# Inverses of two of six row tiles on GpSimd, VectorE's kept in PSUM, in a three-part kernel on one core

## The chip, the core and the metric

The kernel runs on one core of one Trainium2 chip. The metric is the device time of one launch in microseconds (us). A time of a profile is that of one execution, counted from the start of its span.

## The reference

Three parts follow one another; the output of one is the input of the next.

```python
# 1. delta rule: 4 batches x 8 heads, S=768 tokens, D=48
for t in range(S):
    y[:, :, t] = einsum('bhd,bhde->bhe', q[:, :, t], state)
    v_old = einsum('bhde,bhd->bhe', state, k_n[:, :, t])
    state = state + beta_t * outer(k_n[:, :, t], v_t - v_old)
# 2. experts: 3072 tokens of 384, 8 experts of 1024, the best one for each token
e_idx = argmax(x @ w_gate + modality_bias[modality_id])
out[mask_e] = gate_w[mask_e] * (relu(x[mask_e] @ w1[e]) @ w2[e])
# 3. dense layer, 384 -> 2048 -> 384, weights given as float64
h = x @ w_in
out = (h * sigmoid(h)) @ w_out
```

## The kernel before

**Attention.** The 768 tokens are six row tiles t = 0..5 of 128 rows; the 32 heads are two halves p of 16. For each tile TensorE finds the products of keys with keys and of queries with keys (`gram`; VectorE masks the latter into `KB`, `keep_reads`, line 347, eight instructions for each tile, called masks below). The delta rule inside a tile needs, for each head, the inverse of unit lower triangular blocks. All 32x32 blocks of a tile stand side by side: `to_lanes` (one 32x32 transpose, line 361) puts them into `L`, `scales` gives the scaled diagonal of the inverse `A`, and `step(t, j)`, j = 0..30, works the inverse out row by row, each step with multiplications into `tmp` and additions into `A`, in two halves so that neighbouring instructions do not depend on each other. `spread` (line 438) transposes `A` back. Then TensorE joins the 32x32 blocks into 64x64 ones (`join`, line 453), and weights, state and outputs of the tile follow (`lower`, `weigh`, `update`, `state`, `read`), with ScalarE keeping each result. Before, VectorE does all six tiles' steps, with `A` in SBUF; GpSimd only clears `A`.

**Router.** After tiles 1, 2, 4 and 5 a `wave` on VectorE takes the logits of the finished tiles, ranks the tokens of each expert and makes the lists of token indices (the work around line 839 to 1126). It uses constants (`lane`, `k128`, `slot`, ...), counted by GpSimd and cast by VectorE.

**Experts.** The first half of the tokens (tiles 0 to 2) is served in five slots of 256 tokens, in 8 chunks of 128 hidden columns each: `first` is nine matrix products in fp32r pieces (line 1252, high and low parts of tokens and weights), relu is ScalarE's, `second` is plain fp32 products (line 1346, four in the trace) into the two PSUM banks `po`. These slots overlap tiles 4 and 5. GpSimd issues the gathers of their tokens (line 1220, `xg`). The second half is served in four slots of 512 tokens, by three fp32r passes (line 1259), each operand split into a high part by ScalarE and a low part by VectorE (line 1216).

**Dense layer.** Six groups of 512 tokens. The float64 weights come in 28 parts, each of which takes VectorE five instructions (lines 1518 to 1527), called fills below.

**The order.** The class `Order` plans all jobs of the attention, the router and slots 0 to 4 (those of 512 tokens come behind): each job has a key, an engine, a cost, jobs that it waits for and a number from PLAN["rank"]; the order in which each engine's instructions are written follows from them. An engine runs its own in the order written. In gaps of TensorE the planner puts `pulse`s, products of ones whose result is never used (line 709).

Of the kernel before, what the change touches and what calls it, by code (L numbers as in the profile page):

```python
# [1862 lines left out]
```

## Time and the profile before

| | us |
|---|---|
| time, median of 3 runs | 936.82 (935.92 to 937.26) |
| time of the profiled execution | 936.33 |
| its span | 934.6 |
| TensorE busy, in the span | 886.9 |
| VectorE busy | 586.4 |
| ScalarE busy | 424.4 |
| GpSimd busy | 84.4 |

The profiled execution's own time stands 1.7 us over its span and 0.5 us under the median. Its mean granted TensorE clock is 0.974 of full. Busy time is the sum over instructions of what an engine worked on; TensorE's contains the pulses. In rows, PE is TensorE, PEld its weight load, DVE VectorE, ACT ScalarE, POOL GpSimd, SP SyncE.

### The profile page before, as it was taken

Reading aid. Unit: us, or ns where it says so; the run is one execution under the profiler, and the core shown is the slowest. Engines: PE = TensorE matmul, PEld = TensorE weight load, DVE = VectorE, ACT = ScalarE, POOL = GpSimd, SP = SyncE. Lnnn points to the kernel's source line nnn. Section 1 sums busy time; section 2 is a strip of 40 time slices with the busy share of each in tenths; the row PEclk is TensorE's granted clock in tenths of the full one; section 3 lists DMA queues with packets and bytes.
Section 4 is the critical chain, followed back from the end, with each engine's and each line's share of the span. In section 5 each row is a group of like instructions: output and inputs, shape, how many; then the busy total and the mean of one; then the engine's idle time right before and its main releaser. Section 6 shows DMA issues by size and latency. Waiting matters only on the chain. (4 is left out here: it accounts for less than half of the span.)

```text
span 934.6 us, 23107 instructions
## 1 busy us (share of the span) xinstructions
PE 886.9 (95%) x9293; PEld 740.8 (79%) x9293; DVE 586.4 (63%) x1671; ACT 424.4 (45%) x832; POOL 84.4 (9%) x85
## 2 busy tenths in 40 slices
PE   7879998987999799999998999999999999999998
PEld 4548888876888577889887888888888888888897
DVE  4999997999934694699963676542443443343332
ACT  4228576854786434456653544332332233233232
POOL 5000000011011134123311000000000000000000
PEclk8899989998999899999998999999999999999999
DMA  8934645646154505565742531030030100100100
GB/s 193 186 103 104 162 101 145 140 114 196 35 138 131 180 9 160 183 224 179 241 152 65 106 78 43 11 58 1 16 53 1 20 15 1 23 11 1 30 6 35
DMA packets 135351, 85.28 MB, mean 91 GB/s; under 512 B 102361, under 2 KB 121447, under 8 KB 135232
## 3 DMA queue, kind: packets, MB, share of 16 engines
q1 hardware_dynamic: 131904, 73.84, 32.0%
q0 software_dynamic: 3328, 9.83, 3.3%
q8 instruction: 76, 1.25, 0.6%
q14 instruction: 43, 0.35, 0.1%
HBM read 70.53 MB, written 14.55 MB: 91 GB/s over the span
## 5 line engine op out<-in xcount | busy, mean ns | idle before, releaser
L1655 PE MATMUL fpo<-fgh,o 128*128 128x512 f32 x480 | 163.0, 396 | 0.0
L1646 DVE TENSOR_TENSOR fq<-fy,fgh 128x512 fp32r<-128x512 f32 x96 | 66.1, 688 | 110.7 <-ACT fgh L1644 105.2
L1642 DVE TENSOR_TENSOR fy<-fph,fy 128x512 f32<-128x512 f32 x96 | 66.2, 690 | 110.2 <-ACT fy L1640 109.9
L1644 ACT CAST fgh<-fy 128x512 fp32r<-128x512 f32 x96 | 59.6, 621 | 130.7 <-PE fpo L1655 99.2
L1640 ACT ACTIVATE fy<-fph 128x512 f32<-128x512 f32 x96 | 57.4, 598 | 124.0 <-PE fph L1637 122.2
L1637 PE MATMUL fph<-fxh,il 128*128 128x512 f32 x288 | 113.4, 394 | 0.0
L1637 PE MATMUL fph<-fxh,ih 128*128 128x512 f32 x288 | 113.3, 393 | 0.0
L1655 PEld LDWEIGHTS fpo<-fgh,o 128*128 128x128 f32 x480 | 90.3, 188 | 21.2
L1655 PE MATMUL fpo<-fq,o 128*128 128x512 f32 x240 | 95.1, 396 | 0.0
L1259 PE MATMUL poe<-w2s,pairs 128*128 128x384 f32 x384 | 78.5, 347 | 4.1 <-ACTq L1490 3.2
L1259 PEld LDWEIGHTS poe<-w2s,pairs 128*128 128x128 f32 x384 | 69.6, 192 | 8.9 <-ACTq L1490 3.5
L416 DVE TENSOR_TENSOR tmp<-A,L 128x126 f32<-128x126 f32 (+20 forms) x336 | 70.5, 251 | 0.9
L422 DVE TENSOR_TENSOR A<-A,tmp 128x126 f32<-128x126 f32 (+20 forms) x336 | 70.3, 250 | 0.0
L1252 PE MATMUL bank<-xh,wRH 128*128 128x256 f32 x240 | 61.0, 331 | 5.7 <-DVE wRH L1308 5.1
L1637 PEld LDWEIGHTS fph<-fxh,ih 128*128 128x128 f32 x288 | 54.2, 188 | 11.9
L1637 PEld LDWEIGHTS fph<-fxh,il 128*128 128x128 f32 x288 | 54.2, 188 | 11.9
L1346 PE MATMUL po<-raw,hs 128*128 128x384 f32 x160 | 62.5, 516 | 0.0
L1637 PE MATMUL fph<-fq,ih 128*128 128x512 f32 x144 | 57.0, 396 | 0.0
L1637 PE MATMUL fph<-fxl,ih 128*128 128x512 f32 x144 | 56.4, 391 | 0.0
L1655 PEld LDWEIGHTS fpo<-fq,o 128*128 128x128 f32 x240 | 45.2, 188 | 10.8
L1252 PEld LDWEIGHTS bank<-xh,wRH 128*128 128x128 f32 x240 | 41.6, 199 | 10.7 <-DVE wRH L1308 5.5
L709 PE MATMUL po<-ones 128*128 128x512 bf16 x103 | 33.3, 428 | 11.7 <-DVE KB L347 5.3
(436 smaller groups left out, 1660.8 us busy)
## 6 DMA issues: line engine op xcount, KB each, us to landing
raw<-in_moe_w_dram SPq DMA_DIRECT2D x72, 384.0 KB
ri<-in_moe_w_in_dram SPq DMA_DIRECT2D x12, 512.0 KB
ro<-in_moe_w_out_dram SPq DMA_DIRECT2D x16, 384.0 KB
vs<-in_vd_dram SPq DMA_DIRECT2D x12, 384.0 KB
KI<-in_kd_dram SPq DMA_DIRECT2D x24, 192.0 KB
Z<-vs SPq DMA_DIRECT2D x24, 192.0 KB
xs<-Y SPq DMA_DIRECT2D x48, 96.0 KB
fy<-ys SPq DMA_DIRECT2D x72, 64.0 KB
```

Source lines behind the costliest of these rows:

```text
L416: nc.vector.tensor_tensor(tv, r[:, :, j : j + 1].to_broadcast([128, c, n]), L[:, j : j + 1, j + 1 :].to_broadcast([128, c, n]), op=ALU.mult,)
L422: nc.vector.tensor_tensor(r[:, :, j + 1 :], r[:, :, j + 1 :], tv, op=ALU.add)
L709: return nc.tensor.matmul(room, dense, dense[:, None, :].to_broadcast([128, 4, 128]), start=True, stop=True).ins
L1252: self.nc.tensor.matmul(ph, a[:, k, :], b[:, k, :], start=(i == 0), stop=(i == 8))
L1259: self.mark = self.nc.tensor.matmul(o, a[:, cs], b, start=(c == 0 and i == 0), stop=(c == self.F - 1 and i == 2)).ins
L1346: nc.tensor.matmul(self.po[b][:, 0:384], v["h"][c % 2][:, 128 * b : 128 * b + 128], self.raw(1, c), start=(c == 0), stop=(c == F - 1),)
L1637: nc.tensor.matmul(ph, a[:, k, fs], b[:, k, :], start=(n == 0), stop=(n == 8))
L1640: nc.scalar.activation(sg, ph, AF.Sigmoid)
L1642: nc.vector.tensor_tensor(gv, ph, sg, op=ALU.mult)
L1644: self.marks = [nc.scalar.copy(gh, gv).ins]
L1646: self.marks.append(nc.vector.tensor_tensor(gl, gv, gh, op=ALU.subtract).ins)
L1655: nc.tensor.matmul(po[k], a[:, rows], b, start=(f == 0 and i == 0), stop=(f == 15 and i == 2))
```

## The change

Tiles 1 and 4 (`lanes="vpvvpv"`) have all their steps, from scaling `L` on, done by GpSimd, with `A` in SBUF and one update of each step (a multiplication into `tmp`, an addition). Tiles 0, 2, 3 and 5 stay on VectorE, but their `A` lies in PSUM, in the experts' two banks `po`: even rows in one, odd rows in the other. TensorE clears them with two products of zeros (`nil`), the diagonal takes two instructions, and `spread` two transposes of half the size. The first product into `po` (slot 0, chunk 0) waits for the spreads of tiles 4 and 5. An update now adds a multiple of one row to the rows below it; before, it was columns.

The counting and casting of the router's constants are jobs of the order, GpSimd's next count waiting for VectorE's cast. Slots 3 and 4 do their second product in three fp32r passes (`passes=(3, 4)`): VectorE makes the low parts of hidden values (`relu_low`) and of weights (`lo(s, c, 1)`), ScalarE the high ones. A pulse has 256 columns in place of 512, and lies in another bank; in the order there are 56 of them, 103 before. All rank numbers, some costs and so the whole order are new.

```diff
-    one=3, pair=(),
+    lanes="vpvvpv", passes=(3, 4),
...
-        kq=198.9, qb=242.4, vs=64.9, kd=1074.8, gr=178.8, gq=-206.4, Gc=265.8, Kc=-543.5, dg=116.5, zero=481.9,
+        kq=-837.5, qb=792.4, vs=95.3, kd=359.6, gr=277.9, gq=1463.3, Gc=-140.5, Kc=-143.2, dg=145.6, zero=168.1,
...
     def clear_inverses(self, t):
-        A = self.st[t]["A"] = self.pools["ln"].tile([128, 32, 32], F32, tag="A", name=f"A{t}", bufs=2)
-        self.nc.gpsimd.memset(A, 0.0)
+        if PLAN["lanes"][t] == "p":
+            A = self.st[t]["A"] = self.pools["ln"].tile([128, 32, 32], F32, tag="A", name=f"A{t}")
+            self.nc.gpsimd.memset(A, 0.0)
+            return
+        self.st[t]["A"] = self.rows
+        for x in self.rows:
+            self.nc.tensor.matmul(
+                x, self.nil, self.dense[:, None, :].to_broadcast([128, 4, 128]), start=True, stop=True
+            )
...
     def step(self, t, j):
...
+        L, A = self.st[t]["L"], self.st[t]["A"]
+        pool = PLAN["lanes"][t] == "p"
+        eng = self.nc.gpsimd if pool else self.nc.vector
...
-        if j < PLAN["one"]:
-            for i in range(j + 1):
-                for L, A in LA:
-                    nc.vector.scalar_tensor_tensor(
-                        A[:, i, j + 1 :], L[:, j, j + 1 :], A[:, i, j : j + 1], A[:, i, j + 1 :], op0=ALU.mult, op1=ALU.add
-                    )
-            return
...
+        c = j + 1
+        if pool:
+            parts = [(A[:, c:, 0:c], A[:, j : j + 1, 0:c], L[:, j, c:, None])]
         else:
-            rows = [(LA[0][0], LA[0][1][:, w : j + 1 : 2]) for w in range(2)]
+            row = A[j % 2][:, j // 2 : j // 2 + 1, 0:c]
+            parts = []
+            for w in (c % 2, j % 2):
+                k = (c + 1 - w) // 2
+                if k < 16:
+                    parts.append((A[w][:, k:, 0:c], row, L[:, j, 2 * k + w :: 2, None]))
...
+            eng.tensor_tensor(tv, row.to_broadcast([128, n, c]), l.to_broadcast([128, n, c]), op=ALU.mult)
             tmps.append(tv)
-        for (_, r), tv in zip(rows, tmps):
-            nc.vector.tensor_tensor(r[:, :, j + 1 :], r[:, :, j + 1 :], tv, op=ALU.add)
+        for (x, _, _), tv in zip(parts, tmps):
+            eng.tensor_tensor(x, x, tv, op=ALU.add)
...
+                add(("st", t, j), "POOL" if PLAN["lanes"][t] == "p" else "DVE", self.step_cost(t, j),
+                    lambda t=t, j=j: self.step(t, j), [("st", t, j - 1)] if j else [("b2", t)])
+            add(("sp", t), "DVE", 2.15, lambda t=t: self.spread(t), [("st", t, 30)])
...
+        for j, (count, cast) in enumerate(router.consts):
+            once(("ci", j), "POOL", 0.25, 0, count, [("cc", j - 1)])
+            once(("cc", j), "DVE", 0.25, 0, cast, [("ci", j)])
...
-            return nc.tensor.matmul(room, dense, dense[:, None, :].to_broadcast([128, 4, 128]), start=True, stop=True).ins
+            return nc.tensor.matmul(room, dense, dense[:, None, :].to_broadcast([128, 2, 128]), start=True, stop=True).ins
...
+        def relu_low(s, c):
+            hh, hl = v["hh"][c % 2], v["hh"][2 + c % 2]
+            nc.vector.scalar_tensor_tensor(hl, v["ph", s, c], 0.0, hh, op0=ALU.max, op1=ALU.subtract)
...
         def second(s, c):
+            if s in PLAN["passes"]:
+                h = v["hh"][c % 2], v["hh"][2 + c % 2]
+                self.second(c, [x[:, 0:384] for x in self.po], *h, self.bufs["h2"][c % 2], self.bufs["l2"][c % 2])
+                return
...
-                    + ([("ev", s - 1, 0, b) for b in range(2)] if s and c == 0 else []) + ([("wv", 2, "idx")] if (s, c) == (0, 0) else []))
+                    + ([("ev", s - 1, 0, b) for b in range(2)] if s and c == 0 else []) + ([("wv", 2, "idx"), ("sp", T - 1), ("sp", T - 2)] if (s, c) == (0, 0) else []))
```

Three places show how the order moves. A row is: source line, operation, output and input names, size, number. First, VectorE at the start of the program (L is the blocks of tile 0, lines 742 to 754 and 770 cast constants, KB are masks). Before:

```order
L742 CAST lane<-lanei 128x128
L742 CAST k_136<-k128i 128x24
L353 COPY G<-G 32x512
L742 CAST k_140<-k256i 128x12
L742 CAST slot<-sloti 128x52
...
L353 COPY G<-G 32x512
L361 STREAM_TRANSPOSE L_309<-G 128x1024
L347 TENSOR_TENSOR KB_106<-bank_128,amask 64x512 x2
L347 TENSOR_TENSOR KB_106<-bank_124,amask 64x512 x2
L347 TENSOR_TENSOR KB_106<-bank_125,amask 64x512 x2
L347 TENSOR_TENSOR KB_106<-bank_126,amask 64x512 x2
L373 RECIPROCAL rn_399<-n_0_354 128x32
```

And with the change:

```order
L770 CAST lane<-lanei 128x128
L770 CAST k_136<-k128i 128x24
L770 CAST k_137<-k256i 128x12
L355 COPY G<-G 32x512
L770 CAST slot<-sloti 128x52
L355 COPY G<-G 32x512
L375 STREAM_TRANSPOSE L_300<-G 128x1024
L770 CAST down<-downi 128x8
L770 CAST V<-tii 128x24
L770 CAST V<-pii 128x24
L387 RECIPROCAL rn_355<-n_0_327 128x32
```

The second copy of diagonals stands ahead of three casts that it stood behind, and the eight masks that stood between L and the first step are gone from there; they and sixteen more now stand behind the spread of tile 0.

Second, GpSimd where it ends tile 4 (A_1374 is its inverse, L_2871 its blocks) and goes on to the first slot's gathers, with the change:

```order
L437 TENSOR_TENSOR tmp_29_0_4070<-A_1374,L_2871 128x60
L440 TENSOR_TENSOR A_1374<-A_1374,tmp_29_0_4070 128x2x30
L437 TENSOR_TENSOR tmp_30_0_4073<-A_1374,L_2871 128x31
L440 TENSOR_TENSOR A_1374<-A_1374,tmp_30_0_4073 128x31
L1246 DMA xg<-xs,gidx_3811 128x384 x6
```

Before, there were only clearings ahead of the same gathers:

```order
L357 MEMSET A_2419 128x1024
L357 MEMSET A_3272 128x1024
L1220 DMA xg<-xs,gidx_3863 128x384 x5
```

So the gathers stand behind the whole of tile 4's 66 instructions.

Third, VectorE in slots 3 and 4 with the change (line 1376 is `relu_low`, 1336 the low part of a weight, 1562 to 1571 are fills); in the order before, no fill stands ahead of the slots of 512 tokens:

```order
L1336 TENSOR_TENSOR pairs<-raw_4265,pairs 128x384
L1376 SCALAR_TENSOR_TENSOR hhl<-bank_127,hhl 128x256
L1336 TENSOR_TENSOR wRH<-raw_4146,wRH 128x384
L1571 TENSOR_TENSOR il<-ri_0f,ih 128x512
L1336 TENSOR_TENSOR pairs<-raw_4265,pairs 128x384
L1562 TENSOR_SCALAR ri_2e<-ri_2_6945 128x512
L1571 TENSOR_TENSOR il<-ri_1f,ih 128x512
L1376 SCALAR_TENSOR_TENSOR hhl<-bank_128,hhl 128x256
```

Each chunk of these slots has three VectorE instructions of its own (before one), and ten of the 28 parts' fills stand between them.

On TensorE, 11 of the gram jobs stand ahead of the first join (before 20), and ahead of the join of tile 5 the experts' chunks are two firsts and no second (before seven firsts and seven seconds).

## Rows read from the trace of the kernel before

**Rows 1.** Six stretches: busy by engine (instructions), clock, DMA share, GB/s.

```profile
0.00:64.50 64.50, 48.90 (x714) 29.23 (x714) 50.41 (x178) 16.10 (x24) 13.11 (x28) 0.89 0.82 174
64.50:261.60 197.10, 178.93 (x4790) 160.17 (x4790) 184.18 (x810) 131.17 (x278) 9.22 (x8) 0.95 0.48 120
261.60:337.40 75.80, 70.67 (x1029) 57.65 (x1029) 39.55 (x127) 45.54 (x102) 10.17 (x11) 0.95 0.47 133
337.40:377.40 40.00, 40.00 (x248) 31.73 (x247) 23.12 (x52) 17.38 (x42) 17.88 (x12) 1.00 0.38 119
377.40:531.00 153.60, 149.40 (x754) 132.79 (x754) 110.58 (x221) 80.96 (x162) 29.59 (x23) 0.98 0.55 164
531.00:934.60 403.60, 398.98 (x1766) 329.28 (x1764) 178.53 (x286) 133.25 (x227) 4.45 (x4) 1.00 0.13 26
```

**Rows 2.** VectorE in time, first and last spread: start, length, line, operation.

```profile
62.44 2.01 DVE L438 STREAM_TRANSPOSE G<-A 128x1024 f32<-128x1024 f32 x1
...
259.49 2.11 DVE L438 STREAM_TRANSPOSE G<-A 128x1024 f32<-128x1024 f32 x1
```

**Rows 3.** VectorE in time, before the first step.

```profile
13.34 0.17 DVE L742 CAST k<-k256i 128x12 f32<-128x12 int32 x1 [4.77 <-POOL k256i L740]
...
16.08 1.92 DVE L361 STREAM_TRANSPOSE L<-G 128x1024 f32<-128x1024 f32 x1
17.92 5.62 DVE L347 TENSOR_TENSOR KB<-bank,amask 64x512 f32<-64x512 f32 x8
...
25.36 0.42 DVE L399 TENSOR_TENSOR L<-L,b 128x256 f32<-128x256 f32 x1
```

**Rows 4.** Groups of VectorE from 25.3 to 62.44: busy, mean ns, idle before.

```profile
L347 DVE TENSOR_TENSOR KB<-bank,amask 64x512 f32<-64x512 f32 x16 | 11.0, 688 | 0.4
...
L388 DVE TENSOR_TENSOR vs<-vs,nt 128x768 f32<-128x768 f32 x2 | 1.9, 958 | 0.1
L361 DVE STREAM_TRANSPOSE L<-G 128x1024 f32<-128x1024 f32 x1 | 1.9, 1911 | 0.0
```

**Rows 5.** GpSimd's groups in the whole span: busy, mean ns, idle before.

```profile
L579 POOL MEMSET KA<- 128x2048 f32 x3 | 5.3, 1804 | 0.0
...
masks.py:199 POOL TENSOR_SCALAR_AFFINE_SELECT ident<-ident 128x128 f32<-128x128 f32 x1 | 0.3, 292 | 0.1
...
masks.py:197 POOL MEMSET ident<- 128x128 f32 x1 | 0.2, 204 | 0.3 <-POOLq L1845 0.3
```

**Rows 6.** Busy time of VectorE in the stretch of the first waves.

```profile
170.13:195.41 25.28, 22.82 (x107) 1.00 0.57 136
```

**Rows 7.** The page's groups, input from PSUM and from SBUF.

```profile
L1646 DVE TENSOR_TENSOR fq<-fy,fgh 128x512 fp32r<-128x512 f32 x96 | 66.1, 688 | 110.7 <-ACT fgh L1644 105.2
L1642 DVE TENSOR_TENSOR fy<-fph,fy 128x512 f32<-128x512 f32 x96 | 66.2, 690 | 110.2 <-ACT fy L1640 109.9
```

**Rows 8.** VectorE in time, two SBUF operands, and one from PSUM.

```profile
216.31 1.01 DVE L1308 TENSOR_TENSOR wRH<-raw,wRH 128x384 fp32r<-128x384 f32 x2
...
220.32 1.02 DVE L1335 TENSOR_TENSOR xl<-bank,xh 128x384 fp32r<-128x384 f32 x2
```

**Rows 9.** Pulses alone in the second stretch: length, TensorE busy, load busy, clock.

```profile
64.50:261.60 197.10, 8.22 (x30) 2.34 (x30) 0.95 0.48 120
```

**Rows 10.** Groups of TensorE from 0 to 64.5 (a written product is two).

```profile
L334 PE MATMUL bank<-KB,KKQ 48*64 48x64 f32 x320 | 12.9, 235 | 4.4 <-DMA KB<-in_qb_dram 1.8 <-DVE KB L347 1.4 <-issue 1.2
L334 PE MATMUL bank<-KKQ 48*64 48x64 f32 x256 | 10.0, 250 | 0.0
L334 PE MATMUL bank<-KB,KRH 48*64 48x64 f32 x64 | 2.1, 220 | 0.0
```

**Rows 11.** TensorE in time, two chunks of a slot.

```profile
333.99 1.46 PE L1346 MATMUL po<-raw,hs 128*128 128x384 f32 x4
334.99 0.58 PE L1252 MATMUL bank<-xh,wRH 128*128 128x256 f32 x1
335.40 0.28 PE L1252 MATMUL bank<-xl,wRH 128*128 128x256 f32 x1
...
336.24 0.28 PE L1252 MATMUL bank<-xh,wRH 128*128 128x256 f32 x1
336.36 1.46 PE L1346 MATMUL po<-raw,hs 128*128 128x384 f32 x4
```

**Rows 12.** The chain that ended last, a run of three-pass products.

```profile
507.97 2.09 PE poe L1259 x12
```

**Rows 13.** Groups of VectorE from 377.4 to 531.

```profile
L1216 DVE TENSOR_TENSOR w2s<-raw,w2s 128x384 fp32r<-128x384 f32 x30 | 16.5, 550 | 10.7 <-ACT w2s L1215 10.7
...
L1525 DVE SCALAR_TENSOR_TENSOR ri_2f<-ri_2f,ri_2e 128x512 f32<-128x512 f32 x4 | 2.7, 684 | 0.0
```

More of the change, by code (lines that the diff above doesn't have):

```diff
@@ L56 @@
+    ex=253.3, n0=40, npre=40, tok=70,
 )
@@ L437, in spread, with step_cost @@
-    def spread(self, t):
-        self.nc.vector.transpose(
-            out=self.gt(t).rearrange("p u c -> p c u"), in_=self.st[t]["A"].rearrange("p r c -> p c r")
-        )
+    def step_cost(t, j):
+        n, c = 31 - j, j + 1
+        if PLAN["lanes"][t] == "p":
+            return (0.7 if j % 8 == 0 else 0.0) + 2 * (0.16 + 0.0021 * n * c)
+        return (0.34 if j % 8 == 0 else 0.0) + sum(2 * (0.068 + 0.00105 * a * c) for a in ((n + 1) // 2, n // 2) if a)
+    def spread(self, t):
+        A, transpose = self.st[t]["A"], self.nc.vector.transpose
+        if PLAN["lanes"][t] == "p":
+            transpose(out=self.gt(t).rearrange("p u c -> p c u"), in_=A)
+        else:
+            for w, x in enumerate(A):
+                transpose(out=self.gt(t).rearrange("p u (n w) -> p w n u", w=2)[:, w], in_=x)
@@ L623, in plan @@
                         [("ln", t, p), ("up", t - 1, p, e), ("ps", t - 1, p, e), ("py", t - 1, p, e)], size=0.8)
[L624 to L630 removed]
+            for j in range(31):
+                add(("st", t, j), "POOL" if PLAN["lanes"][t] == "p" else "DVE", self.step_cost(t, j),
+                    lambda t=t, j=j: self.step(t, j), [("st", t, j - 1)] if j else [("b2", t)])
+            add(("sp", t), "DVE", 2.15, lambda t=t: self.spread(t), [("st", t, 30)])
             for p in range(2):
@@ L686, in wave @@
         half = self.T // 2
-        needs = [("gt", t, 3)]
+        needs = [("gt", t, 3), ("tris",)] + [("cc", j) for j in range(len(router.consts))]
         if t % half == half - 1:
@@ L775, in __init__, with triangles @@
         self.total = cp.tile([128, E], BF16, name="total")
+    def triangles(self):
+        nc, E = self.nc, self.E
+        nc.gpsimd.memset(self.low, 1.0)
+        nc.gpsimd.affine_select(
+            out=self.low, in_=self.low, pattern=[[1, E], [-1, E]], compare_op=ALU.is_gt, fill=0.0, base=0,
+            channel_multiplier=0,
+        )
+        nc.gpsimd.memset(self.tri, 1.0)
+        nc.gpsimd.affine_select(
+            out=self.tri, in_=self.tri, pattern=[[1, 128]], compare_op=ALU.is_gt, fill=0.0, base=0,
+            channel_multiplier=-1,
+        )
     def load(self):
@@ L1277, in open @@
             b["h1"], b["l1"] = ([rest(x, 128) for x in ws[k : k + 2]] for k in (0, 2))
+        if what == "p":
+            self.v["hh"] = cut(ar.tile([128, 1024], F32R, tag="KQ1", name="hhl"), [256] * 4)
         if what == "o":
@@ L1356, in before @@
             return [(name, k // F, k % F, b)] if 0 <= k < F * S else []
+        done = [("gt", T - 1, 3)] + [("out", T - 1, p, e) for p in range(2) for e in range(2)]
         for s in range(S + 1):
```

203 lines of the change are left out of this document (96 added, 107 removed).

## The prediction

> **What bounds the kernel now.** I read the stretches first [rows 1]. From 0 to 64.5 VectorE and TensorE work side by side and neither is full, but VectorE's row of spreads has a first at 62.4 and a last at 259.5, its end at 261.6 [rows 2]. Between them VectorE is busy for 184.2 of 197.1 us, TensorE for 178.9, of which 8.2 are pulses [rows 9]. So up to the join of tile 5 VectorE leads, with TensorE close behind: its real work there is 170.7. Behind the last spread it turns: TensorE is busy for 70.7 of 75.8, then 40.0 of 40.0, 149.4 of 153.6 and 399.0 of 403.6, VectorE for less than six tenths of each, but for 110.6 of 153.6 in the slots of 512 tokens. What counts is when the last join can run, and how much TensorE work is left behind it.
>
> **VectorE's chain up to the last spread.** Before, the transpose of L(0) starts at 16.1, behind casts that wait for GpSimd's counts (one sat from 8.6 to 13.3 for it), and eight masks of 5.6 stand between it and the scales; the first step starts at 25.4 [rows 3]. After, fewer casts stand ahead, so I start L(0) at 12.5 (an estimate: GpSimd reaches that count one or two 1.8 us clearings earlier [rows 5]); with 1.9 for it and 1.8 for the scales (23.5 to 25.4) the first step starts at 16.2.
>
> One tile's steps cost 21.8: from 25.36 to the spread at 62.44 are 37.1, less 16 masks with their idle time (11.4), two value rows (1.9), L(1) (1.9) and a small clearing (0.1) [rows 2 to 4]. The change has 122 instructions a tile for updates in place of 112 and 6 of another kind; I add 0.4, and 1.0 for PSUM (below). Tile 0 is done with L(1) and the scales of tile 1 (3.7) and a spread (2.0) at 45, where it was 64.5.
>
> Next stand 24 masks (16.5 at 0.69), four value rows (3.8), four copies and five bias operations (4.0, estimated by their sizes) and L(2) (1.9): 71.4. Then the spread of GpSimd's tile 1.
>
> **GpSimd's time for a tile** is the disputed cost: no row of before shows it doing arithmetic of two operands. It has 66 instructions over 2x5,456 + 1,024 = 11,936 elements. Low bound: one pass at a clearing's 0.88 ns an element (1,804 ns for 2,048), nothing more than 0.09 fixed, 16.5 us. One operand read over a clearing costs (292 − 204)/128 = 0.69 ns [rows 5]; two reads give 2.26 ns an element, 27.0, and 0.2 fixed for each of 66 gives 13.2: T = 40. High bound: three whole passes (2.64) and 0.29 fixed, 50.7. I take 40, since reading two operands is nearest to the row that reads one.
>
> Tile 1 starts on GpSimd when its scales are done, half way through tile 0's steps, at about 29.5, and is done at 69.5: hidden behind the 71.4. Spread, 73.5. Tile 2 (1.8 + 23.2 + 2.1) ends at 100.6; tile 3, with L(3), L(4), two masks, two value rows (34.4), at 135.0. Tile 4 starts on GpSimd at 137.8 and ends at 177.8. VectorE has for that time the first wave, 22.8 [rows 6], 14 masks (9.6), three value rows (2.9) and L(5) (1.9), to 175: it waits 3. The slot's gathers, behind tile 4 on GpSimd, are late for VectorE's two low parts of tokens, but not for the join: firsts were filling, not leading. Behind it stand a spread (2.1), eight masks (5.5), two low parts (1.0) and scales (1.8), 188; tile 5's steps with two low parts and a logit (24.5) and its spread (2.1): **215**, where it was 261.6.
>
> **PSUM for A.** An operand from PSUM costs 690 ns against 688 at 512 elements [rows 7], so an instruction by itself costs the same. But steps hide each other's fixed part by overlapping: two instructions with SBUF operands took 1.01, two with one from PSUM 1.02 [rows 8], hence no loss there; masks, all from PSUM, came 0.70 apart (5.62/8) and last 0.69 [rows 3, 4], hence no overlap at all. Bounds: 0 to 0.09 us for each instruction. I take 0.01 (1.0 a tile), because the pair of [rows 8] has two independent updates in a row as the steps have.
> [...]
>
> **TensorE's floor.** Its real work from 64.5 to 261.6 is 170.7. Added: nine gram jobs of the first stretch that now come behind tile 0, 25.0/20 each [rows 10], 11.3. Taken away: five firsts (1.08 each: eight fill 0.96 from 335.40 to 336.36) and seven seconds (2.37 − 1.08 = 1.29) [rows 11] that now stand behind the join, 14.4. So 167.6 behind 45: the join of tile 5 can't come before **213**. VectorE's 215 is so near that the two will catch each other: before, TensorE lost 18 of 197 with VectorE leading by a little. I take 222.
>
> **Behind the join.** Before, 115.8 from 261.6 to the slots of 512 (377.4). Added are the 14.4. The three passes of slots 3 and 4 save 1.29 − 6 x 0.177 [rows 12] = 0.23 in each of 16 chunks, −3.7. That is 126.5 of TensorE's work, at full speed. But VectorE has in these two slots 16 low parts of hidden values (0.42, as 256 elements in [rows 3]), 38 of weights and tokens (0.55) and 48 fill pieces (0.58, an estimate: three of 0.68, two of 0.42) [rows 13]. In a row each starts 0.09 sooner than the one ahead ends (two of 0.55 take 1.01 [rows 8]), so 16 x 0.33 + 38 x 0.46 + 48 x 0.49 = 46.3 against 16 x 2.14 = 34.2 of TensorE. If nothing hides, 12 are lost; but the stretch before has VectorE idle for nearly half, and low parts can be made two chunks ahead. I take 5. The slots of 512 start at 222 + 126.5 + 5 = **353.5**, which is 24 earlier.
>
> **The rest.** Slots of 512 tokens lose the fills pulled ahead, 48 x 0.58 = 28 us of VectorE's 110.6, where TensorE waits 4.2 in all; I take 1 of it. The dense layer, with 4.6 not busy, stays. Shorter pulses cost nothing while the clock of the stretches stays at 0.89 and 0.95 [rows 1]; a fall of 0.05 over the first 45 would be 2.
>
> **Sum:** 936.3 − 24 − 1 = 911.3 in the profiled execution's terms; the median of the runs lies 0.5 above that execution. I say 911. A difference of 0.2% (1.9 us) is about what can be told from no change.
>
> **Rivals.**
> - *TensorE is the floor.* GpSimd nearer its low bound and no waits: the join of tile 5 at 213, the extra VectorE work of slots 3 and 4 hidden, 339.5, and up to 4 us saved behind: about 895. For it: TensorE has work in store at every point of the stretch; against it: both engines have to be on time all along.
> - *GpSimd is dearer*, T from 48 to 55: tile 1 is no longer hidden (+6 to +13) and tile 4 adds 8 to 15 more; the spread of tile 5 comes at 229 to 243, and the kernel gives 917 to 934. Another way there: masks, value rows with two SBUF operands and the wave stand beside GpSimd's steps, and the two engines may hold each other up. No row of before has them both on such work.
> [...]
> - *No change.* At T near 57 all that tile 0 and the start bring is lost again: 936. It asks for a GpSimd above my high bound.
> - *Slower: PSUM takes the overlap away.* If each of 488 instructions costs 0.09 more, as the spacing of masks would have it, the four tiles lose 44 us in series, tile 5's spread comes at 259, and with the 14.4 and the 5 still to pay behind it the slots of 512 start near 390: about 948. It breaks even at 63 ns an instruction. For it: masks; against it: the pair of [rows 8].
>
> **How the numbers follow.** Forecast, 903 to 920: 0.50. TensorE's floor, 893 to 903: 0.18. GpSimd dearer, 920 to 934: 0.18. No change: 0.04. Slower: 0.10. Leaving out the slower one, no change and what lies at the edges gives 893 to 932 as the range. Faster 0.86, same 0.04, slower 0.10.
>
> **What would show it.** The spread of tile 0 ending near 45; the first GpSimd tile taking about 40 with the spread of tile 1 not waiting; tile 2 of VectorE from scales to spread in 25 to 26 (above 30: PSUM costs overlap); VectorE's wait for tile 4 at most a few us; the spread of tile 5 between 213 and 225; TensorE waiting 5 or so for `relu_low` or weights' low parts in slots 3 and 4; the slots of 512 starting near 353; the dense layer again 403.6. Wrong it would be made by T far from 40, by VectorE and GpSimd blocking each other, and by a lower granted clock now that pulses are fewer and half as long.

## The result: 0.3 to 0.5% slower, and the profile after

Eight runs of each gave 942.87 us (938.58 to 945.21) against 937.40 (935.75 to 941.33): a ratio of 1.0051, 95% interval 1.0028 to 1.0073. Twelve runs on another chip gave 1.0026 (1.0000 to 1.0052). Forecast were 911 and a range of 893 to 932. The prediction is wrong, in its sign too.

The page of the changed kernel, profiled execution 943.61 us, span and granted clock by slices:

```profile
span 941.5 us, 23018 instructions
PEclk9769998797999999999998999999999999999999
```

Its stretches (columns as in [rows 1]), cut at the same events: end of the spread of tile 0, join of tile 5, first product of the 512-token slots, end of their last, end.

```profile
0.00:50.80 50.80, 32.22 (x404) 22.52 (x405) 36.13 (x165) 16.62 (x24) 24.33 (x52) 0.84 0.81 167
50.80:247.10 196.30, 183.97 (x5022) 170.94 (x5021) 166.00 (x600) 126.31 (x268) 69.92 (x113) 0.88 0.57 137
247.10:380.30 133.20, 124.40 (x1355) 104.55 (x1351) 92.90 (x248) 78.99 (x179) 27.48 (x23) 0.96 0.43 129
380.30:536.20 155.90, 149.09 (x745) 133.55 (x746) 95.07 (x188) 75.14 (x151) 28.41 (x23) 0.98 0.51 144
536.20:941.50 405.30, 400.33 (x1766) 329.36 (x1764) 178.53 (x286) 133.28 (x227) 4.32 (x4) 1.00 0.14 25
```

Beside [rows 1]: the join of tile 5 comes 14.5 earlier (247.1 for 261.6), where 39.6 were forecast. From it to the slots of 512 are 133.2 (before 115.8; forecast 131.5), these slots take 155.9 (153.6; 152.6), the dense layer 405.3 (403.6; 403.6). So 25 of the 32 us by which the forecast missed lie ahead of that join, and there the reader should look at the clock: 0.84 and 0.88, where [rows 1] has 0.89 and 0.95, and at TensorE, busy for 184.0 of 196.3, more than VectorE.

VectorE's spreads (start, length):

```profile
48.89 1.93 DVE L455 STREAM_TRANSPOSE G<-po 128x512 f32<-128x512 f32 x2
...
81.75 1.91 DVE L452 STREAM_TRANSPOSE G<-A 128x1024 f32<-128x1024 f32 x1
...
106.95 1.91 DVE L455 STREAM_TRANSPOSE G<-po 128x512 f32<-128x512 f32 x2
...
145.17 1.99 DVE L455 STREAM_TRANSPOSE G<-po 128x512 f32<-128x512 f32 x2
...
203.58 1.97 DVE L452 STREAM_TRANSPOSE G<-A 128x1024 f32<-128x1024 f32 x1
...
243.25 2.05 DVE L455 STREAM_TRANSPOSE G<-po 128x512 f32<-128x512 f32 x2
```

The ends forecast were 45, 73.5, 100.6, 135, 180 and 215; they are 50.8, 83.7, 108.9, 147.2, 205.6 and 245.3. What was lost lies in four gaps: the start (+5.8), spread 0 to 1 (+4.4), 2 to 3 (+3.9), and 3 to 5, +13.4 and +4.7. Tile 2, whose steps run with nothing beside them, was even 1.9 faster than forecast. Now TensorE in time, at the start:

```profile
6.11 0.61 PE L729 MATMUL ranks<-ones 128*128 128x256 bf16 x2 [3.65 <-ACT KI L304]
...
9.49 0.61 PE L729 MATMUL ranks<-ones 128*128 128x256 bf16 x2 [1.06 <-ACT KI L304]
10.03 7.09 PE L336 MATMUL bank<-KKQ 48*64 48x64 f32 x128
...
41.46 0.40 PE L729 MATMUL ranks<-ones 128*128 128x256 bf16 x1 [8.99 <-DVE po L440]
```

Pulses stand in TensorE's queue ahead of the grams and wait there for ScalarE's unit rows (L304), which come late. The first gram runs at 10.0 (before, 4.8), and 128 of its products take 7.09 us, 55 ns each, where before they took 3.95, 31 ns each:

```profile
4.80 3.95 PE L334 MATMUL bank<-KKQ 48*64 48x64 f32 x128
```

At 32.5 TensorE runs dry for 9 us, since the next pulse waits for a step of VectorE. Three stretches of the same trace, clock in the third column from the right:

```profile
34.00:61.00 27.00, 16.94 (x180) 10.87 (x182) 24.57 (x97) 3.63 (x6) 21.28 (x39) 0.50 0.37 68
157.00:177.00 20.00, 19.47 (x347) 17.90 (x347) 11.43 (x36) 7.46 (x18) 18.04 (x28) 0.50 0.66 144
207.00:225.00 18.00, 16.93 (x308) 15.37 (x310) 14.11 (x63) 7.81 (x18) 0.00 (x0) 0.54 0.87 226
```

For 65 us TensorE goes at about half clock (0.50, 0.50 and 0.54). Each stretch begins in or right behind idle time of TensorE: 9.0 us before 41.5, 2.1 at 155.4, 2.1 at 205. GpSimd's two tiles, first and last instruction (the second row gives the idle time since the end of tile 1):

```profile
36.89 0.72 POOL L419 TENSOR_TENSOR L<-L,b 128x256 f32<-128x256 f32 x1 [15.71 <-DVE b L396]
...
83.73 0.95 POOL L365 MEMSET A<- 128x1024 f32 x1 [4.23 <-DVE G L452]
149.86 0.72 POOL L419 TENSOR_TENSOR L<-L,b 128x256 f32<-128x256 f32 x1 [65.18 <-DVE b L396]
...
193.80 0.25 POOL L440 TENSOR_TENSOR A<-A,tmp 128x31 f32<-128x31 f32 x1
```

So T is 42.6 and 44.2, near the 40 taken. VectorE beside tile 4, in time:

```profile
167.04 0.23 DVE L923 TENSOR_TENSOR rk<-ranks,OH 128x64 f32<-128x64 f32 x1 [6.33 <-PE ranks L915]
...
172.28 0.59 DVE L905 COPY cb<-ca 128x8 bf16<-128x8 bf16 x1
```

The same copy of eight elements, as a group of the kernel before, from 170 to 262:

```profile
L879 DVE COPY cb<-ca 128x8 bf16<-128x8 bf16 (+1 forms) x3 | 0.5, 171 | 0.1
```

Summed over the first wave's rows, its 98 instructions last 27.7 us, and 99 of them 20.4 before. Between the spreads of tiles 3 and 4 VectorE also waits five times, for 10.8 us in all, 6.3 of it behind TensorE's ranks in the second half-clock stretch. GpSimd has finished at 194.05; the spread starts at 203.58. So VectorE comes last there by 9.5, where the forecast had it wait 3 for GpSimd.

### The profile page after: what moved, and what is told of

Its sections match the earlier page's. It is cut to its first block, busy times and chain, and to the rows that moved or that the text cites. A ratio compares the mean times of both kernels' runs of the same rounds, so it can differ in the third digit from the quotient of the medians.

```text
span 941.5 us, 23018 instructions
## 1 busy us (share of the span) xinstructions
PE 890.0 (95%) x9286; PEld 760.9 (81%) x9286; DVE 568.6 (60%) x1482; ACT 430.3 (46%) x846; POOL 154.5 (16%) x213
## 5 line engine op out<-in xcount | busy, mean ns | idle before, releaser
L1278 PE MATMUL bank<-xh,wRH 128*128 128x256 f32 x240 | 56.6, 314 | 6.3 <-DVE wRH L1336 6.3
L1699 PEld LDWEIGHTS fpo<-fq,o 128*128 128x128 f32 x240 | 45.1, 188 | 10.8
L1246 POOL DMA_INDIRECT xg<-xs,gidx x26 | 30.9, 1187 | 119.8 <-PE bank L1260 83.5
L440 DVE TENSOR_TENSOR po<-po,tmp 128x126 f32<-128x126 f32 (+35 forms) x244 | 50.4, 253 | 0.1
L437 DVE TENSOR_TENSOR tmp<-po,L 128x126 f32<-128x126 f32 (+35 forms) x244 | 49.5, 245 | 0.5
L1278 PE MATMUL ph<-pairs,wRH 128*128 128x512 f32 x144 | 38.1, 402 | 0.0
```

The lines of the kernel that those rows point to most:

```text
L437: eng.tensor_tensor(tv, row.to_broadcast([128, n, c]), l.to_broadcast([128, n, c]), op=ALU.mult)
L440: eng.tensor_tensor(x, x, tv, op=ALU.add)
L1246: self.nc.gpsimd.indirect_dma_start(out=rows, out_offset=None, in_=self.xs[0 : self.xs.shape[0] // (2 - n), :], in_offset=bass.IndirectOff ...
L1278: self.nc.tensor.matmul(ph, a[:, k, :], b[:, k, :], start=(i == 0), stop=(i == 8))
L1699: nc.tensor.matmul(po[k], a[:, rows], b, start=(f == 0 and i == 0), stop=(f == 15 and i == 2))
```

## The experiments

e1 to e4, e5 to e8, e9 to e12 and e13 to e16 ran beside each other, each group on one chip with the kernel before between them; executions of one kernel differ there by some 1%, so ratios count. A ratio is to the kernel before on the same chip, whose median was 933.7 to 934.6 in these four groups; 937.4 belongs to the row of the changed kernel. Milestones are of one profiled execution each. A mark behind `#` in a diff names the runs that have the lines and is not in the code.

| run | time | ratio (95%) | first gram | spread 0, 5 | join 5 | 512 slots | span |
|---|---|---|---|---|---|---|---|
| before | 937.4 | 1 | 4.8 | 62.4, 259.5 | 261.6 | 377.4 | 934.6 |
| changed | 942.9 | 1.0028 to 1.0073 | 10.0 | 48.9, 243.2 | 247.1 | 380.3 | 941.5 |
| e1 | 934.9 | 0.9987 to 1.0042 | 10.0 | 48.6, 235.1 | 237.9 | 369.3 | 928.5 |
| e2 | 941.6 | 1.0046 to 1.0110 | 10.6 | 52.7, 245.8 | 248.3 | 378.7 | 938.8 |
| e3 | 972.0 | 1.0328 to 1.0435 | 7.9 | 46.2, 276.5 | - | 411.0 | 970.6 |
| e4 | 935.2 | 0.9982 to 1.0042 | 10.0 | 48.9, 245.1 | 247.6 | 378.0 | 933.5 |
| e5 (changed again) | 936.9 | 1.0000 to 1.0052 | 10.0 | 47.7, 241.4 | 243.8 | 375.4 | 936.2 |
| e6 | 930.7 | 0.9942 to 0.9993 | 10.0 | 48.3, 238.3 | 241.5 | 372.3 | 928.7 |
| e7 | 930.5 | 0.9933 to 0.9986 | 10.2 | 50.0, 240.7 | 243.2 | 374.5 | 931.6 |
| e8 | 943.0 | one run | 10.0 | 53.0, 244.8 | 247.3 | 380.6 | 940.9 |
| e9 | 935.7 | 0.9976 to 1.0026 | 10.5 | 50.5, 245.1 | 247.5 | 378.9 | 935.6 |
| e10 | 924.5 | 0.9853 to 0.9924 | 6.9 | 45.6, 233.6 | 236.0 | 366.8 | 922.4 |
| e11 | 927.4 | 0.9890 to 0.9948 | 6.3 | 45.4, 237.6 | 240.4 | 369.9 | 925.6 |
| e12 | 971.9 | 1.0352 to 1.0470 | 10.5 | 44.1, 269.9 | 273.6 | 413.8 | 968.3 |
| e13 | 922.5 | 0.9860 to 0.9911 | 6.9 | 44.0, 234.7 | 237.1 | 367.1 | 924.6 |
| e14 | 929.4 | 0.9942 to 0.9998 | 7.0 | 45.3, 232.6 | 235.1 | 365.4 | 927.1 |
| e15 | 937.0 | 1.0012 to 1.0057 | 5.0 | 43.8, 241.2 | 243.6 | 375.5 | 936.9 |
| e16 (e10 again) | 926.6 | 0.9891 to 0.9949 | 6.4 | 44.3, 236.0 | 238.5 | 369.1 | 926.6 |

**e1 and e2: stronger pulses.**

```diff
-            return nc.tensor.matmul(room, dense, dense[:, None, :].to_broadcast([128, 2, 128]), start=True, stop=True).ins
+            x = [nc.tensor.matmul(room, dense, dense[:, None, :].to_broadcast([128, 2, 128]), start=True, stop=True) for _ in range(2)]   # e2: range(4)
+            return x[0].ins
-                x = max(at + 0.02, j["start"] - 9.0)
+                x = max(at + 0.02, j["start"] - 20.0)   # e2 only
```

> The changed kernel with each pulse as two products of 256 columns, so 512 as before; the order is the same. Theory A (TensorE leads up to the last join and its granted clock, 0.84 and 0.88 there against 0.89 and 0.95 before, is what the weaker pulses cost): the stretch from 34 to 61 at half clock gets shorter by a third or more, the join of tile 5 comes at 235 to 243 where it is 247.1, time 930 to 939. Theory B (VectorE and GpSimd lead, with GpSimd at 43 to 44 us a tile and VectorE's small instructions beside it taking 0.4 to 0.6 us where they took 0.2): clock and time stay, 943 within 2.

> The changed kernel with four products of 256 columns for a pulse, and pulses allowed in the 20 us ahead of a planned job where it was 9. Theory A: no half clock between 34 and 61, the grams behind the first join run at 0.031 us in place of 0.056 a product, the spread of tile 1 at 75 in place of 81.8, the join of tile 5 at 225 to 238, time 918 to 935. Theory B: as without it, 943 within 2, or slower, if pulses stand in front of real work.

In e1 the same 128 gram products, TensorE in time, and the first half-clock stretch:

```profile
10.04 3.95 PE L336 MATMUL bank<-KKQ 48*64 48x64 f32 x128
```

```profile
34.00:61.00 27.00, 18.19 (x324) 13.36 (x325) 26.41 (x98) 5.59 (x10) 21.57 (x39) 0.81 0.36 81
```

The products go at 31 ns again, the clock is 0.81 in place of 0.50. Theory A holds; its size is less than the first profile said (13 us): over three profiles with these pulses and the start as it was (e1, e6, and e7, whose moved load left the first gram where it was) the join is at 237.9 to 243.2, without (changed, e5, e4) at 243.8 to 247.6, 5 us on average. In time the pulses by themselves are not clear of the noise (e1 1.0014, the changed kernel 1.0051 and 1.0026). What is clear is e14 against e15, on one chip and with the untied start in both, the pulses alone being different: 0.9970 (at most 0.9998) against 1.0034 (at least 1.0012), the join at 235.1 against 243.6.

TensorE's busy time from the spread of tile 0 to the join, less pulses, says the same without the waits: 179 to 184 us in the five profiles with pulses of 256 columns (changed, e4, e5, e8, e15), 170 to 178 in the nine with 512 (e1, e6, e7, e9, e10, e11, e13, e14, e16), for the same 5,015 to 5,017 products.

e2 is the other side, and misses theory A: its pulses kept the clock at 1.00 from 35 to 85 (e1: 0.50 to 0.80 from 35 to 50, then 1.00) but wait for jobs of other engines in front of real work; L(1) comes at 34.7 in place of 30.9, the first join at 59 in place of 52, the join of tile 5 at 248.3.

**e3 and e7: keys ahead of values.** e3 takes out the empty job `("boot",)` ahead of the keys in the plan; e7 leaves the plan and moves only the load, on top of e6.

```diff
-                        [("boot",)] + [(g, *ring(t, p, len(self.K)), k) for g in ("gr", "gq") for k in range(2)], size=1.9 / len(us))   # e3
+                        [(g, *ring(t, p, len(self.K)), k) for g in ("gr", "gq") for k in range(2)], size=1.9 / len(us))
-                    add(("kq", t, p, i), "SP", 0.8, lambda t=t, p=p, x=x: self.fetch(t, p, x),   # e7
+                    add(("kq", t, p, i), "SP", 0.8, lambda t=t, p=p, i=i, x=x: (self.fetch(t, p, x), (t, p, i) == (0, 1, 1) and self.fetch_values(0, 0)),
-                add(("vs", t, p), "SP", 0.58, lambda t=t, p=p: self.fetch_values(t, p),
+                add(("vs", t, p), "SP", 0.58, lambda t=t, p=p: t + p > 0 and self.fetch_values(t, p),
```

> The changed kernel without the empty job ahead of the keys' loads, so that the first keys are loaded ahead of the first values, as before the change; the order is solved again. The first gram comes at 5 to 7 in place of 10.0 and L(0) at 13 to 15 in place of 18.4. If the start is passed on (both theories have it lead): 935 to 939. If a later wait swallows it: 943 within 2.

> As the run with 512-column pulses and without the three passes, and the load of the first values issued behind the first tile's keys on SyncE's queue, nothing else moved. If the values' load is what keeps the first gram at 10.0: the gram at 6 to 8, L(0) at 12 to 13 where that run has about 15.3, time 2 to 4 us less. Rival (the pulses that wait for ScalarE's unit rows, and stand ahead of the grams on TensorE, keep it): gram at 10.0 and no change in time.

e3 tells little of the load: 1.2 us less in the plan gave another order altogether, with waits of 9.2 and 3.5 us for copies by DMA, and 30 us more. e7 moved the load alone, and the first gram stayed at 10.15: the rival, the waiting pulses, was right.

**e4 and e6: no three passes,** alone and with e1's pulses; e5 is the changed kernel beside it.

```diff
-    lanes="vpvvpv", passes=(3, 4),
+    lanes="vpvvpv", passes=(),
```

> The changed kernel with slots 3 and 4 in plain products again (no three passes); nothing moves ahead of tile 5's join. Theory P (the low parts and the fills make VectorE the bound in these slots, which was full from 343.6 to 391.9): first product of the 512-token slots at 375 to 378 in place of 380.3, time 938 to 941. Rival (the three passes save their 3.7 us of TensorE and the fills alone do the harm): 946 to 947.

> The changed kernel with both edits at once: pulses of 512 columns and slots 3 and 4 in plain products. Theory A with theory P (the clock ahead of the last join, and VectorE's extra low parts in slots 3 and 4, are two separate losses): their gains of 13 and 8 us in the profiled executions add up, span near 920, ratio to before 0.980 to 0.988. Rival (one bound stands behind both, so that the second gain finds nothing): span 926 to 934, ratio 0.993 or more.

> The changed kernel unaltered, beside the next three on one chip. Every theory: its ratio to before is 1.003 to 1.007, as it was.

The changed kernel in the stretch of slots 3 and 4, and e4 in that of the slots of 512 tokens (columns of [rows 1]):

```profile
343.60:391.90 48.30, 40.87 (x245) 36.65 (x243) 48.30 (x104) 33.45 (x74) 12.24 (x9) 0.96 0.63 202
```

```profile
378.00:527.60 149.60, 146.34 (x737) 130.98 (x736) 85.70 (x167) 72.25 (x146) 26.28 (x23) 0.99 0.49 141
```

VectorE is busy for all of the 48.3 us, TensorE for 40.9: VectorE leads there. Without the passes the time from the join to the dense layer falls from 289.1 to 280.0. Most of that is lost behind the two slots: the slots of 512 tokens take 155.9 in the changed kernel with 188 instructions on VectorE, and 149.6 with 167 in e4. With the passes they take 153.3 to 156.5 (changed, e1, e2, e5, e8, e14, e15), without 149.6 to 151.6 (e4, e6, e7, e9 to e11, e13, e16); from the join to them are 130.3 to 133.3 and 129.5 to 131.4.

e6 meets its rival's numbers (span 928.7, ratio 0.9967), not those of two gains that add up. But the single gains were far smaller than single profiles said: by ratio e1 and e4 are worth 0.1 to 0.4% each, and e6 stands 0.6% under e5, some 5.5 us, where the 13 and 8 of the profiles would make 2.2%. So nothing here speaks for one bound behind both; the intervals are too wide to show the sum.

**e8: even rows in SBUF, odd rows in PSUM.**

```diff
-        self.st[t]["A"] = self.rows
-        for x in self.rows:
-            self.nc.tensor.matmul(
-                x, self.nil, self.dense[:, None, :].to_broadcast([128, 4, 128]), start=True, stop=True
-            )
+        x = self.pools["ln"].tile([128, 16, 32], F32, tag="Av", name=f"Av_{t}")
+        self.st[t]["A"] = [x, self.rows[1]]
+        self.nc.vector.memset(x, 0.0)
+        self.nc.tensor.matmul(
+            self.rows[1], self.nil, self.dense[:, None, :].to_broadcast([128, 4, 128]), start=True, stop=True
+        )
```

> The changed kernel with the even rows of VectorE's inverses in an SBUF tile (cleared by VectorE, 0.3 to 0.6 us a tile) and the odd rows left in PSUM, so that one execution has both kinds of step instruction side by side. Theory of no cost: where GpSimd is at rest (tiles 2, 3, 5) a step instruction on SBUF rows and one on PSUM rows last the same within 10 ns, tile 2 from scales to spread again takes 21.6. Rival of the prediction (PSUM takes overlap away): the SBUF rows are faster by 60 ns or more. [...]

VectorE's groups of steps from 37 to 53, while GpSimd works on tile 1 (mean ns behind the comma; Av is in SBUF, po in PSUM):

```profile
L441 DVE TENSOR_TENSOR Av<-Av,tmp 128x120 f32<-128x120 f32 (+14 forms) x16 | 6.1, 383 | 0.0
L438 DVE TENSOR_TENSOR tmp<-Av,L 128x120 f32<-128x120 f32 (+15 forms) x16 | 5.4, 369 | 0.1
L441 DVE TENSOR_TENSOR po<-po,tmp 128x126 f32<-128x126 f32 (+15 forms) x17 | 4.3, 256 | 0.0
L438 DVE TENSOR_TENSOR tmp<-po,L 128x128 f32<-128x128 f32 (+7 forms) x16 | 3.3, 241 | 0.0
```

And from 86 to 110.2, tile 2, GpSimd at rest:

```profile
L441 DVE TENSOR_TENSOR po<-po,tmp 128x126 f32<-128x126 f32 (+22 forms) x31 | 7.9, 255 | 0.1
L441 DVE TENSOR_TENSOR Av<-Av,tmp 128x110 f32<-128x110 f32 (+20 forms) x30 | 7.2, 240 | 0.0
L438 DVE TENSOR_TENSOR tmp<-Av,L 128x16 f32<-128x16 f32 (+30 forms) x31 | 6.3, 244 | 0.1
L438 DVE TENSOR_TENSOR tmp<-po,L 128x30 f32<-128x30 f32 (+7 forms) x30 | 6.1, 244 | 0.0
```

At rest PSUM costs 15 ns in the additions, of which some 5 are size (an estimate: 92 elements on average against 87, at the 1.05 ns an element by which 512 elements, 690 ns in [rows 7], last longer than 256, 420 in [rows 3]), and nothing in the multiplications. Beside GpSimd an instruction with both inputs in SBUF lasts 383 and 369 ns, 0.13 us more than one with an input in PSUM, whose 256 and 241 are those at rest (255 and 244). Both the prediction's slower rival and the idea that `A` in PSUM buys nothing fall.
The wave pays too: its 98 instructions last 27.7 us in the changed kernel and 29.6 in e10, and the same 98 last 20.1 in e12 (below), where GpSimd has no tile. So GpSimd's steps cost 7 to 9 us there. No TENSOR_REDUCE or RECIPROCAL of these rows is longer by 0.1; what is longer are TENSOR_TENSORs with their inputs in SBUF, and also, at some places and not at others, COPYs, CASTs and TENSOR_SCALARs, which read one tensor (a COPY of eight elements takes 0.59 us at 172.3 in the changed kernel, and 0.17 at 155.3 as in the kernel before; a CAST of eight 0.34 to 0.45 for 0.18, a TENSOR_SCALAR of eight 0.45 for 0.17).

**e9 to e11: masks, start, longer pulses,** on e6.

```diff
+        later = max(j["start"] for j in o.jobs if j["key"][:2] == ("Kc", 4))   # e9, e11
+        for j in o.jobs:
+            if j["key"][:3] == ("Kc", 5, 1):
+                j["start"] = later + 0.01 * (1 + j["key"][3])
+        o.line.sort(key=lambda j: j["start"])
-                    out.append((x, behind[-1] if behind else None))   # e10, e11
+                    out.append((x, behind[-1] if behind and x > 9.0 else None))
-                x = max(at + 0.02, j["start"] - 9.0)   # e11
+                x = max(at + 0.02, j["start"] - 16.0)
```

> On the run with 512-column pulses and without the three passes: four masks of tile 5 (half of the eight that stand between L(5) and the spread of tile 4 on VectorE) moved behind that spread; nothing else. GpSimd's tile 4 is done some 5 to 9 us before the spread that waits behind them. Theory S (the spread of tile 4 stands on the chain and is late by VectorE's own order, not by GpSimd): spread of tile 4 2.8 earlier, TensorE's idle time near 205 shorter and its clock there higher, join of tile 5 3 to 8 earlier, time 927 to 929 by the scale on which that run had 930.7. Rival (tile 5's own work waits for those masks, or TensorE's backlog covers all): no change.

> On the same run: the pulses that the plan puts into the first 9 us no longer wait for ScalarE's unit rows. Theory (those waits on TensorE's queue, at 6.1, keep the first gram at 10.0, where it was 4.8 before the change): first gram at 6 to 8, L(0) at 12 to 13, and 2 to 4 us of it at the end. Rival (the keys' load keeps it): gram at 10.0.

> On the same run: both of those edits, and pulses in the last 16 us of a planned gap where it was 9, so that the idle 9 us between 32 and 41 are filled. Theory A: no half clock from 20 to 50 but for single stretches of 5, gains add: 5 to 10 us less than the run it stands on. Rival: pulses that wait for VectorE's steps hold real work up, as with pulses of 1,024 columns, and the first join comes late.

In e9 and e11 the moved masks act on values that are not those of the reference, the instructions being the same. e9 brought nothing. Its spread of tile 4 came 51.4 behind that of tile 3, where e1, e6 and e7 have 52.6 to 53.8, although the other masks then waited 1.8 us for TensorE. But from there to the spread of tile 5 it took 44.4, where they have 38.6 to 40.3: its rival, that tile 5's own work waits for those masks, fits. e10 is the gain:

```profile
6.87 3.95 PE L336 MATMUL bank<-KKQ 48*64 48x64 f32 x128
```

The gram comes 3.2 earlier, every spread 2.7 to 6.2 earlier than in e6, and the ratio falls from 0.997 to 0.989 (e16, the same again: 0.992). e11 adds nothing to it (0.992): its longer filling lifts the clock to 0.95 from 35 to 40 and 1.00 from 40 to 45, where e10 has 0.50 and 0.65, but the spread of tile 1 comes at 76.6 for 76.8, and its moved masks cost it 3 us between the spreads of tiles 4 and 5, as in e9.

**e12: no tile on GpSimd,** on e6.

```diff
-    lanes="vpvvpv",
+    lanes="vvvvvv",
```

> On the same run: all six tiles on VectorE, in PSUM, GpSimd none; the order is solved again (which alone moved 30 us when the keys' loads were moved in the plan, so only the stretches of a tile are compared). Theory (moving two tiles to GpSimd shortens the chain, by 22 us for tile 1 and by what VectorE has to do beside it for tile 4): the stretch from the spread of tile 0 to that of tile 5 is 20 to 45 us longer. Rival (the chain does not get shorter, TensorE is the bound): it is within 10.

From the spread of tile 0 to that of tile 5 are 225.8, in e6 190.0, in e10 188.0: 36 us of chain, as the theory has it. It is no clean price of moving two tiles, since e12's order is solved again: the kernel before, also with all six tiles on VectorE, takes 197.1 there, with 24 masks fewer in the stretch (16.5 by the prediction's count). VectorE is busy for 195.7 of e12's stretch and 166.3 of e6's, so the two tiles take 29 us of work off it. The copy of eight elements, with GpSimd at rest in e12 from 165 to 270:

```profile
L906 DVE COPY cb<-ca 128x8 bf16<-128x8 bf16 (+1 forms) x3 | 0.5, 172 | 0.1
```

**e13 to e16: what is left.** e13 adds sixteen untied products in front of TensorE's idle time near 195, e14 puts the three passes back, e15 is the untied start alone.

```diff
+        at = next(j["start"] for j in self.line if j["key"] == ("ps", 3, 1, 1))   # e13
-        line += [(x, 1, n, k) for n, (x, k) in enumerate(self.pulses(until))]
+        line += [(x, 1, n, k) for n, (x, k) in enumerate(self.pulses(until) + [(at - 0.01, None)] * 8)]
```

> On the run with 512-column pulses, no three passes and the untied start: sixteen products of 256 columns, waiting for nothing, in TensorE's queue at the place near 195 where it sits idle for 1.9 us for masks and its clock then falls to half until 216. Theory A (the clock there delays the join): no half clock between 197 and 216, join of tile 5 3 to 8 earlier than 236, time 917 to 922. Rival (VectorE leads there, TensorE catches up in any case, or the clock falls even so): join within 2 of it, same time.

> 512-column pulses and the untied start, with the three passes in slots 3 and 4 as the change has them. Theory P (the passes cost some 5 us, since VectorE and ScalarE make their parts in slots where they lead): 3 to 7 us slower than the same without passes. Rival (they cost nothing when the join comes earlier): within 1.5 us.

> The changed kernel with the untied start alone (pulses of 256 columns, three passes). Theory: first gram at 5.5 to 7, in place of 10.0, but at half pace if the weak pulses leave the clock low; L(0) at 14 to 16, time 2 to 4 us less than the changed kernel's, ratio to before 0.998 to 1.002. Rival (the start's gain is taken up by the next wait): ratio 1.003 or more.

> The run with 512-column pulses, no three passes and the untied start once more, beside these: ratio to before 0.985 to 0.993 as it was.

e13's filling ran (TensorE in time), and the clock still was 0.50 from 205 to 215 and 0.73 in the 5 us behind (e10: 0.50 and 0.75), and the join stayed at 237:

```profile
197.61 1.92 PE L730 MATMUL ranks<-ones 128*128 128x256 bf16 x16
```

e14 against e10, e13 and e16: 0.997 for 0.989 to 0.992, so the passes cost 0.5 to 0.8%, 5 to 8 us. e15 is the telling one. Its first gram is not at half pace, as its expectation feared:

```profile
4.99 4.28 PE L336 MATMUL bank<-KKQ 48*64 48x64 f32 x128
```

The stretch from 29 to 62 in e15, then in e16, clock third from the right:

```profile
29.00:62.00 33.00, 23.07 (x295) 16.82 (x296) 29.58 (x104) 5.09 (x10) 26.77 (x47) 0.51 0.49 90
```

```profile
29.00:62.00 33.00, 23.64 (x522) 18.67 (x519) 32.27 (x110) 8.69 (x17) 26.27 (x47) 0.84 0.59 119
```

In e15 the spread of tile 0 comes 5 earlier than in the changed kernel, at 43.8, but then tile 1's comes at 80.4, 36.6 later, where e16 needs 31.2: the masks wait for grams at half clock, and the whole start is given back (1.0034, the rival of its expectation). With the wider pulses the same edit is worth 0.5 to 0.8%.

## Why the prediction was wrong, by its own steps

- **TensorE's floor and the pulses: "Shorter pulses cost nothing while the clock of the stretches stays at 0.89 and 0.95".** This is the step that failed. The condition did not hold (0.84, 0.88), and its price if not, 2 us over the first 45, was too small. The floor of 213 was worked out with products at the old clock: real work between the spread of tile 0 and the join took 182 (184.0 less 1.8 of pulses) for the 167.6 forecast. That is 14.6 of the 25 us by which the join missed; 5.8 are the start, and the other 4.7 are pulses and idle time (14.1 for the 9.4 that lie between 212.6 and 222). With pulses of 512 columns the same work takes 170 to 178, so 4 to 12 of the 14.6 are shown to be the pulses' doing. At the join they are worth some 5 us (e1, e6, e7), and together with the untied start 9 to 10 (e10, e13, e14, e16: 235.1 to 238.5, for 243.8 to 247.6). So the pulses are a good part of the miss, and not the whole of it.
- **The start, L(0) at 12.5.** It came at 18.4: I looked at VectorE's queue and not at TensorE's, where pulses now wait for ScalarE ahead of the first gram. e7 and e10 show which wait it was; untied, L(0) comes at 13.1.
- **The first wave beside tile 4, 22.8.** That was VectorE's busy time in a stretch. Like for like, the wave's instructions last 20.4 before, 27.7 in the changed kernel, 29.6 in e10 and, without a tile on GpSimd, 20.1 in e12: GpSimd's steps hold VectorE up. I had it as a rival and did not price it in the sum. In e10, e13, e14 and e16 the spread of tile 4 still comes 52.1 to 53.6 behind that of tile 3, where 45 were forecast; these 7 to 9 us are about half of what is left between their 235 to 238.5 and the 222. The other half is not taken apart.
- **GpSimd's T, 40:** 42.6 and 44.2, right. **PSUM, 0.01 an instruction:** 0 to 0.015 in e8, right.
- **Behind the join:** 133.2 for 131.5, right as a sum. But of the slots of 512 tokens I had only a gain, 152.6; they took 155.9, and 149.6 to 151.6 without the passes. So the passes, taken as 3.7 saved and 5 lost, lose 5 to 8 on the whole, most of it in the slots behind them. Why VectorE's work there grows was not followed further.
- **The slower rival** was put on PSUM, which was innocent. What made it slower had no place in the list: a weaker filler, and fillers that wait (e14, without both, is at 0.997), and passes that cost more than they save (e4, without them, is at 1.001).

Open: the half clock of some 10 to 20 us that begins between 195 and 215 in every run that keeps the changed kernel's order, and that one filling did not cure; 1.7 to 2.4 us more in the dense layer, which nothing in the change explains; and how much of executions' spread on one chip is a matter of where such stretches fall.

The best version is e10, the change with pulses of 512 columns, plain products in slots 3 and 4, and an untied start: in e10, e13 (with its harmless filling) and e16 0.8 to 1.1% faster than the kernel before. That is still short of the 2.8% forecast.

## What to carry to other kernels

A sum of TensorE's work held here at one clock only (the same products up to the join of tile 5 took 179 to 184 us with pulses of 256 columns, 170 to 178 with 512): where a change thins out what keeps TensorE busy in gaps, price the work behind the gap at half clock too (0.50 to 0.54 for 65 us of the changed kernel). Filler work has a place in a queue: here the grams stood behind fillers that waited for another engine (first gram at 10.0, and at 6.9 in e10 without those waits), so look at the filler's waits in the order before and after. And work moved to GpSimd was not free for VectorE here: of the instructions that run beside it, count those with two SBUF inputs (383 and 369 ns in e8, for 240 and 244 at rest), and copies, casts and operations with a scalar (up to 0.59, 0.45 and 0.45 us of eight elements, for 0.17 to 0.18), at their slower time.

## What was not expected of the hardware

- At the start of a run, 128 gram products took 7.09 us in the changed kernel, where TensorE had been busy for 4.1 of the 10.0 us ahead of them; 3.95 in e1 (6.2 of 10.0); and 4.28 in e15, with the narrow pulses again but none that waits (3.8 of 5.0). The granted clock read 1.00 all the same (10 to 15 in the changed kernel): there the pace of products shows what that column does not.
- A copy of eight elements took up to 0.59 us beside GpSimd's steps (0.17 at another place) and 0.17 without; 98 instructions of a wave 27.7 to 29.6 us beside them and 20.1 without.
- TensorE stayed at half clock for 18 to 20 us while busy for 94 to 97% of that time (157 to 177, 207 to 225).
